# A long convolution with a gated dense block: products and inverse by 128 channels, D added ahead of the transposes, a new order

## The chip, the cores and the metric

The kernel runs on one core of a Trainium2 chip. The core has five engines that run side by side, each with its own queue of instructions: TensorE (PE in the profile, its weight loads PEld), VectorE (DVE), ScalarE (ACT), GpSimd (POOL) and SyncE (SP, which here only issues DMA transfers). Matmul results go to PSUM, from where DVE or ACT must copy them to SBUF before the PSUM tile can be used again; such a copy is called an eviction. The metric is the device time of one execution in microseconds (us), less is better. The inputs and the output are in HBM and of type bfloat16.

## The reference

Sequence length S = 2048, channels D = 640, hidden width F = 1728, batch 1.

```python
# part A: a gated long convolution
k_shift[s, d] = sum over t < 4 of k[s - 3 + t, d] * shift_k[d, 3 - t]
kv   = k_shift * v
y_f  = rfft(pad(kv, 4096)) * rfft(pad(ssm_k, 4096))      # along the sequence, by channel
y    = irfft(y_f)[:S].astype(bfloat16) + kv * ssm_D
A    = layernorm(q) * y                                   # no weights, eps 1e-5
h    = q + A
# part B: a dense block
u    = layernorm(h) @ w1 + b1                             # 640 -> 1728
act  = u * tanh(softplus(u))                              # Mish
out  = h + act @ w2                                       # 1728 -> 640
```

## The kernel before

The Fourier transform of length 4096 is taken in two stages, as matrix products with tables from HBM. The channels are split into five groups of 128 (`dc` or `m` = 0 to 4). Since y = irfft(...) + D·kv, D is added to the filter's first sample ahead of its transform.

**Order.** Every step is a named operation (`OP`) with an engine, its inputs and, where it needs one, a PSUM tile. The text `ORDER` (L25 to L60) lists all operations in the order in which they are emitted, and so sets the order of each engine's queue. `name@2` puts the operation in PSUM tile 2 of the four tiles of 128 x 1024 f32; a tile is free when the eviction of its former content is done. `name:d`, `:a` or `:p` puts an eviction (or a scaling) on DVE, ACT or POOL instead of its usual engine. An eviction is `ev` (L245), on ACT in L247 and on DVE in L249.

**The stages**, with the operations' names and lines:

- Loads (L302, on SP's queue): the filter rows (`d_n`, five of 512 KB), the first-stage table `g` (`d_g`), `k` and `v` (`d_k`, `d_v`), later q (`d_x`) and the weights. Small loads on ACT's queue: the constants (`d_cst` L255), the taps (`d_sk` L256), D as one row of 640 (`d_dr` L257). `wm` (L269) are nine warm-up matmuls.
- Filter: `k1pe` (L352) transposes a group's filter, 16 transposes of 128x128; `k1ev` evicts 2,048 columns; `dadd` (L359) adds D to the first sample, one row, on POOL; `s1kpe` (L374, L375) is the first stage, 16 pairs of matmuls into half tiles for each quarter of a group; `s1kev` evicts 1,024 columns.
- Short convolution and product: `ktpe` (L318) transposes k, `ktev` evicts it, `ktsh` (L322, POOL) shifts it by one, `kspe` (L334, L335) applies the taps (whose table is `coef` L286 and `wsh` L294), `kv` (L339, DVE) multiplies by v out of PSUM.
- Value: `s1vpe`, `s1vev` are the first stage of `kv`.
- Second stage (L400): `s2k` for the filter, all five groups in one matmul of 160 columns for each of 128 frequencies, evicted in tiles of 960; `s2v` for the value, by chunks of groups (`CHUNKS`: group 0, groups 1 and 2, groups 3 and 4), so with 32 or 64 columns.
- `sw` (L432): ten transfers of 512 KB from SBUF to SBUF that swap the real and the imaginary rows of the transformed filter. `pr` (L443, DVE): 20 products of filter and value, 2,048 elements a partition each.
- First inverse stage `i1pe` (L464), 20 operations of 16 matmuls, `i1ev` evicts 1,024 columns of each. An `i1pe` waits for all the products of its chunk.
- Second inverse stage `i2pe` (L519), for each of 16 tiles of 128 tokens (t): eight matmuls over 640 channels; `y` (ACT) evicts.
- Around it, by tile t: `ln1` (L495, L496, DVE) takes the statistics of q, `ln1p` (L500 to L502, POOL) the inverse deviation, `lnx` (L507 ACT or L509 POOL) the normalized q; `wb` (L522) and `h` (L524) multiply and add, `bn` (L528 to L530) takes h's statistics, `pow` (L532, POOL) the inverse deviation, `hc` (L534) scales; the result is transposed on PE (`trpe` L543, evicted by `trev`; tiles 0 and 1) or by a DMA (`tr` L547, the others).
- Dense block by units of tokens (`UNITS`: 256, 256, 512, 512, 512): `m1pe` (L570; L573 for the last 64 rows of F, block 13, whose two halves of tokens go to two halves of the partitions) and `hb` (L581, ACT, Mish); `m2pe` (L612, L620) for each tile of tokens, `res` (L635, DVE; L632 for the last tile, in two parts of 512 and 128 columns) adds h; `d_out` (L639) stores.

Ten of the 16 `ln1` stand ahead of the second inverse stage (two of them beside the products), and all 16 `i2pe` ahead of the first `m1pe`.

Of the kernel before, what the change touches and what calls it, by code (L numbers as in the profile page):

```python
# [11 lines left out]
ALU = mybir.AluOpType  # L12
BF16 = mybir.dt.bfloat16
# [3 lines left out]
S = 2048  # L17
# [20 lines left out]
s1vpe1_1@0 s1vev3_2 s1vpe1_0@1 s2v0pe_96@3 d_x0 s1vev1_0 pr0_32 sw1_00 s2v0pe_64@2 s1vev1_1 sw1_10 s2v0ev_96:d sw1_01 s1vpe2_0@1 s2v0ev_64 d_t2m
s1vpe2_1@0 pr0_96 sw2_00 s1vpe3_0@3 s1vev2_0 s2v0pe_0@2 d_x1 pr0_64 sw2_11 s1vev2_1 sw2_10 s2v0ev_0 ln1_3 s2v1pe_112@1 kspe4_1@0 s1vev3_0 sw2_01 pr0_0
ln1p3 s2v1pe_32@2 s2v1pe_16@3 s2v1ev_32 ln1_1 lnx3:p s2v1ev_16 s1vpe3_1@2 kv4_1 ln1p1 s2v1ev_112 s2v1pe_48@3 s2v1pe_64@0 s1vev3_1 s2v1ev_48:d lnx1:p  # L40
s2v1pe_96@1 s2v1ev_64 s2v1pe_0@2 pr1_48 s1vpe4_0@3 s2v1ev_96 s1vpe4_1@0 pr1_64 s2v1ev_0 s1vpe4_3@1 s1vev4_0:d s1vev4_1 s1vpe4_2@2 s1vev4_2 pr1_96
s2v1pe_80@0 i1pe0_0@3 s1vev4_3 pr1_112 s2v1ev_80 s2v2pe_32@2 pr1_16 i1ev0_0 s2v2pe_64@1 s2v2pe_0@0 pr1_32 s2v2ev_32 s2v2pe_96@3 s2v2ev_0 s2v2ev_64:d
s2v2pe_48@2 s2v2ev_96 s2v2pe_16@0 pr1_0 s2v2pe_80@1 s2v2ev_48 i1pe0_2@3 pr1_80 s2v2ev_16 s2v2pe_112@2 pr2_64 s2v2ev_80 i1pe0_1@0 pr2_48 d_w14
s2v2ev_112 d_x2 i1pe1_3@1 i1ev0_1 d_x3 pr2_32 d_w12 i1pe1_6@2 i1ev1_3 d_w10 pr2_80 d_w13 i1pe1_0@0 i1ev1_6 d_w11 pr2_16 i1pe1_5@1 i1ev0_2 i1pe1_4@2
pr2_96 i1ev1_0 i1pe0_3@3 i1ev1_4 pr2_112 i1pe1_2@0 i1ev1_5 pr2_0 i1pe1_7@2 i1ev1_2 i1pe1_1@1 ln1_2 i1ev0_3 i1pe2_6@0 ln1_4 i1ev1_7 ln1p2 i1pe2_5@3
i1ev1_1 ln1_12 ln1p4 i1pe2_7@2 i1ev2_5 ln1_0 i1pe2_0@1 lnx4:p i1ev2_6 ln1_8 i1pe2_1@3 lnx2:p i1ev2_7 i1pe2_3@0 ln1p0 i1ev2_0 i1ev2_1:d i1pe2_4@2
i1ev2_3 ln1_5 ln1p8 i1pe2_2@1 i1ev2_4 ln1_6 lnx0:p d_w2c i1ev2_2 d_w2b ln1_7 ln1p12 d_w2a i2pe0@3 i2pe1@0 y0 ln1p5 i2pe3@2 y1 wb0 i2pe9@1 y3 wb1 ln1p6
i2pe4@3 y9 h1 i2pe6@0 y4 bn1 i2pe7@2 y6 i2pe10@1 y7 h0 i2pe2@3 pow1 bn0 y10 i2pe12@0 ln1p7 y2 i2pe8@2 wb3 y12 i2pe11@1 pow0 hc1 i2pe13@3 y8 h3 trpe1@0
y11 lnx8:p i2pe5@2 hc0 y13 trev1 trpe0@1 wb2 i2pe15@0 trev0:a h2 i2pe14@3 bn3 y15 m1pe0_5@1 y5 bn2 pow3 m1pe0_4@0 hb0_5 w2z y14 hc3 m1pe0_2@2 ln1_11
# [111 lines left out]
def kernel(  # L161
# [25 lines left out]
    banks = [psum.tile([P, 1024], F32, name=f"ps{i}") for i in range(4)]  # L187
    big = ctx.enter_context(tc.tile_pool(name="big", bufs=1))

    cst = cpool.tile([P, 4 * P + 32], BF16, name="cst")  # L190
    sk_r = cpool.tile([32, 80], BF16, name="sk_r")
    coef = cpool.tile([P, 20, 7], BF16, name="coef")
    st1 = cpool.tile([P, NT, 2, 6], F32, name="st1")
# [487 lines left out]
```

## Time and profile before

| | us |
|---|---|
| three runs | 228.24, 310.08, 228.19 |
| median | 228.24 |
| profiled execution, its own time | 227.79 |
| its span (first to last instruction of the profile) | 226.0 |
| busy: PE, weight load, DVE, ACT, POOL | 214.5, 161.2, 133.8, 134.0, 56.6 |

The granted clock of TensorE is 1.00 in the whole span. Read the busy times by stretch, not over the span: PE, DVE and ACT are loaded differently in the convolution (to about 100 us) and in the dense block (after it). An instruction of PE, ACT or DVE begins before its predecessor's recorded end, so the time that one more instruction takes is the spacing of the starts, which is a little less than the recorded mean duration. "Idle before, releaser" names what ended the wait of an engine.

### The profile page before, as it was taken

What the parts mean: (1) busy time and instruction counts of PE and PEld (TensorE: products, weight loads), DVE (VectorE), ACT (ScalarE), POOL (GpSimd) and SP (SyncE); (2) the same over time, 40 slices, a digit from 0 to 9 for tenths busy, and PEclk for the clock granted to TensorE, in tenths of its full rate; (3) what the DMA queues carried; (4) which work ended last, traced back from release to release, by engine and by line L of the source; (5) the groups of instructions that cost most, each with busy time, mean ns of one, the idle gap of its engine ahead of it and who ended that gap; (6) DMA issues with size and microseconds to landing.
All of it is one profiled execution on the core that took longest, in us unless ns stands there. A gap on an engine that the chain in (4) does not pass through costs nothing.

```text
span 226.0 us, 6327 instructions
## 1 busy us (share of the span) xinstructions
PE 214.5 (95%) x2758; PEld 161.2 (71%) x2764; DVE 133.8 (59%) x240; ACT 134.0 (59%) x184; POOL 56.6 (25%) x103
## 2 busy tenths in 40 slices
PE   7999999998888999799899999999999999999994
PEld 2898999998778999788787654444667444666762
DVE  0576877898999999799999999500020200021041
ACT  2688899999999999999795004745500164300000
POOL 4377230000650018866847204100000000000000
PEclk9999999999999999999999999999999999999999
DMA  7999980049993959101301352820001100000102
GB/s 219 378 419 405 411 348 7 3 165 325 402 418 109 408 201 331 45 3 29 32 1 32 80 151 51 105 55 0 0 3 58 58 3 0 0 33 28 58 29 87
DMA packets 19421, 31.01 MB, mean 137 GB/s; under 512 B 10689, under 2 KB 14786, under 8 KB 18626
## 3 DMA queue, kind: packets, MB, share of 16 engines
q1 hardware_dynamic: 19104, 30.46, 39.5%
q8 instruction: 21, 0.34, 0.6%
q10 hardware_dynamic: 194, 0.15, 0.2%
q14 instruction: 6, 0.05, 0.1%
q0 software_dynamic: 96, 0.00, 0.0%
HBM read 20.45 MB, written 2.62 MB: 102 GB/s over the span
## 4 chain that ended last, share of the span: by engine, by line
PE 69%; ACT 15%; DMA 8%; DVE 3%; issue 2%; POOL 1%; SPq 1%; ACTq 0%; POOLq 0%; DVEq 0%
PE ps L612 25%; PE ps L570 22%; ACT uv L247 11%; DMA ra<-in_A_k_dram 5%; PE ps L400 5%; PE ps L464 5%; DMA ks<-in_A_ssm_k_dram 3%; PE ps L318 2%; PE ps L334 2%; PE ps L374 2%; ACT ks L581 2%; PE ps L335 2%; PE ps L620 1%; PE ps L573 1%; ACT ra L507 1%
## 5 line engine op out<-in xcount | busy, mean ns | idle before, releaser
L581 ACT ACTIVATE ks<-ps,b1s 128x512 bf16<-128x512 f32 (+1 forms) x70 | 35.9, 598 | 49.1 <-PE ps L570 16.9
L612 PE MATMUL ps<-ks 128*128 128x320 bf16 (+2 forms) x419 | 58.4, 299 | 0.1
L570 PE MATMUL ps<-G 128*128 128x512 bf16 (+1 forms) x320 | 57.6, 336 | 0.9 <-ACT ks L581 0.6
L612 PEld LDWEIGHTS <-ks 128*128 128x128 bf16 x420 | 40.2, 98 | 17.8 <-issue 1.3
L635 DVE TENSOR_TENSOR rb<-ps,rb 128x640 bf16<-128x640 f32 x15 | 11.9, 819 | 67.4 <-PE ps L620 65.1
L570 PEld LDWEIGHTS <-G 128*128 128x128 bf16 x325 | 31.1, 98 | 25.4 <-issue 2.0
L247 ACT CAST uv<-ps 128x1024 bf16<-128x1024 f32 x52 | 48.1, 1181 | 0.4 <-PE ps L375 0.2
L247 ACT CAST ks<-ps 128x960 bf16<-128x960 f32 (+3 forms) x50 | 41.1, 902 | 3.3 <-PE ps L375 1.3
L443 DVE TENSOR_TENSOR ks<-ks,uv 128x2048 bf16<-128x2048 bf16 x20 | 23.2, 1215 | 0.7 <-DMA ks<-ks 0.7
L400 PEld LDWEIGHTS <-G 128*128 128x128 bf16 x512 | 21.1, 96 | 3.3 <-issue 2.8
L464 PE MATMUL ps<-a_t,ks 128*128 128x128 bf16 x320 | 18.8, 219 | 0.3 <-ACT uv L247 0.3
L464 PEld LDWEIGHTS <-ks 128*128 128x128 bf16 x320 | 18.3, 113 | 0.5 <-issue 0.3
L500 POOL TENSOR_SCALAR ve<-mv 128x1 f32<-128x1 f32 x16 | 4.9, 308 | 46.7 <-DVE mv L496 45.6
L400 PE MATMUL ps<-uv,G 128*128 128x64 bf16 (+1 forms) x384 | 13.2, 187 | 2.1 <-ACT uv L247 1.8
L532 POOL TENSOR_TENSOR r<-ve,mhalf 128x1 f32<-128x1 f32 x16 | 10.2, 643 | 18.1 <-DVE ve L530 18.1
L528 DVE BATCH_NORM_STATS2 st<-rb 128x6 f32<-128x320 bf16 x32 | 14.1, 481 | 0.1
L339 DVE TENSOR_TENSOR ra<-ps,rb 128x1024 bf16<-128x1024 f32 x10 | 12.2, 1219 | 2.7 <-PE ps L335 2.7
L495 DVE BATCH_NORM_STATS2 st<-rb 128x6 f32<-128x320 bf16 x32 | 13.7, 471 | 0.0
L374 PE MATMUL ps<-cst,ra 128*64 128x128 bf16 x160 | 10.8, 220 | 1.3 <-ACT uv L247 1.1
L400 PE MATMUL ps<-ks,G 128*128 128x160 bf16 x128 | 11.2, 231 | 0.1
L249 DVE CAST ks<-ps 128x1024 bf16<-128x1024 f32 (+1 forms) x8 | 9.4, 1202 | 2.9 <-PE ps L375 1.9
L374 PE MATMUL ps<-cst,ks 128*64 128x128 bf16 x160 | 10.6, 220 | 0.4 <-POOL ks L359 0.4
(65 smaller groups left out, 259.3 us busy)
## 6 DMA issues: line engine op xcount, KB each, us to landing
ks<-ks SPq DMA_DIRECT2D x10, 512.0 KB, 7.2
G<-tab_g SPq DMA_DIRECT2D x8, 512.0 KB, 11.2
ks<-in_A_ssm_k_dram SPq DMA_DIRECT2D x5, 512.0 KB, 6.1
ra<-in_A_k_dram SPq DMA_DIRECT2D x4, 640.0 KB, 10.8
rb<-in_A_v_dram SPq DMA_DIRECT2D x4, 640.0 KB, 11.2
rb<-in_A_q_dram SPq DMA_DIRECT2D x4, 640.0 KB, 6.1
out_dram<-rb SPq DMA_DIRECT2D x15, 160.0 KB, 1.8
G<-in_B_w_dram SPq DMA_DIRECT2D x5, 432.0 KB, 7.9
```

The source lines that it names most:

```text
L247: nc.scalar.copy(o, i)
L339: nc.vector.tensor_tensor(kv_w[:, m, :, 8 * h:8 * h + 8, :], p_.f32().rearrange("p (l t d) -> p d t l", l=4, t=8), raw_v[:, 8 * h:8 * h + ...
L374: nc.tensor.matmul(ps[0:64, dgl, :], lhs, mc, start=True, stop=True)
L400: nc.tensor.matmul(p_.f32()[:, o:o + n], g_v[:, f, :], src[:, :, f, :], start=True, stop=True)
L443: nc.vector.tensor_tensor(o, o, v, ALU.mult)
L464: nc.tensor.matmul(pz[:, dgl, :], KS[:, k, b, :, l], a12[:, k, :], start=k == 0, stop=k == 1)
L495: nc.vector.bn_stats(st1[:, t, hh, :], xt(t)[:, hh * 320:(hh + 1) * 320])
L528: nc.vector.bn_stats(st2[:, t, hh, :], xt(t)[:, hh * 320:(hh + 1) * 320])
L570: nc.tensor.matmul(ph[:, o:o + w], w1[:, dc, fc * P:fc * P + P], lt[:, dc, 0:w], start=dc == 0, stop=dc == NDC - 1)
L581: nc.scalar.activation(hb[:, fc, 0:n], p_.f32()[:, i * 512:i * 512 + n], ACT.Mish, bias=b1s[:, fc:fc + 1], scale=1.0)
L612: nc.tensor.matmul(p_.f32()[:, o:o + n], lhs, w2[:, k, cols:cols + n], start=fc == 0, stop=single and fc == 13)
L635: nc.vector.tensor_tensor(x, p_.f32().rearrange("p (a d) -> p a d", a=2)[:, :, 0:320], x, ALU.add)
```

## The change

1. **D ahead of the transposes.** The identity for the transposes is no longer loaded with the constants, but made by POOL. D is loaded as 20 values for each of 32 groups of channels, repeated for four partitions; DVE picks its own value for each partition (`lane`, `dsel`, `dcol`) and adds it to the filter's first column before the transposes. The transposes begin with sample columns 1 to 15; column 0, which holds the sum, comes last. The five additions on POOL go.
2. **Halved first eviction.** The first filter group's eviction (`k1ev0`) is in two halves, and each quarter of its first stage waits for its half alone.
3. **Chunks** of the value's second stage: groups 0 to 2 (96 columns) and groups 3 and 4 (64 columns). That is 256 matmuls instead of 384, evicted in 13 tiles of 960 or 768 and 8 of 1,024 columns.
4. **Products and first inverse stage by group of 128 channels.** Still 20 products of 2,048 elements; an `i1pe` waits for the four products of its own group. The inverse's buffer is laid out by groups, so that `i2pe` has four matmuls (two of 512 columns, two of 128) instead of eight, over the same 1,280 columns.
5. **Split second inverse stage** for tiles 0 to 3: `i2a` (groups 0 to 3) waits for the evictions of these groups alone, `i2b` for the last group.
6. **Units 0 and 1 merged in part**: block 13 of F of both units is computed together in `m1pe1_6`, and the second dense layer of tiles 0 to 3 is done in one set that waits for both units.
7. **Last tile** in parts of 384 and 256 columns instead of 512 and 128.
8. **A new order of everything.** Of the `ln1`, four stand beside the value's stages (ahead of the products), four among the `i1pe`, two among the first `i2pe` and six beside the `m1pe` of units 0 and 1. Tiles 8 and 11 have their `i2pe` behind the `m1pe` of unit 1, the other 14 ahead of the first `m1pe`. More evictions are on DVE: for the filter's first stage 8 instead of 6, the value's first stage 6 instead of 4, `s2k` 6 instead of 2; `s2v` 2 instead of 3; one `ktev` moves from DVE to ACT.

```diff
-CHUNKS = [[0], [1, 2], [3, 4]]
+CHUNKS = [[0, 1, 2], [3, 4]]
...
-SW_PIECES = 2
+SW_PIECES = 1
...
+I2S = (0, 1, 2, 3)
+K1S = (0,)
...
+D_FIRST = True
+MERGE = True
+BY_DC = True
...
-    d_dr = OP("d_dr", "actq", emit=lambda e: nc.scalar.dma_start(d_row, A_ssm_D.unsqueeze(0)))
+    d_dr = OP("d_dr", "actq", emit=lambda e: nc.scalar.dma_start(dful[:], A_ssm_D.rearrange("(d n) -> d n", n=20).unsqueeze(1).to_broadcast([32, 4, 20])))
+
+    def emit_id(e):
+        nc.gpsimd.memset(ident, 0.0)
+        nc.gpsimd.affine_select(out=ident, in_=ident, compare_op=ALU.not_equal, fill=1.0, base=0, pattern=[[-1, P]], channel_multiplier=1)
+    o_id = OP("idn", "pool", emit=emit_id)
+    o_ln = OP("lane", "dve", [o_id], emit=lambda e: nc.vector.tensor_reduce(lane[:], ident.rearrange("p (d l) -> p l d", l=4), axis=AX.X, op=ALU.max))
...
     for b in range(NDC):
+        dad = OP(f"dadd{b}", ["dve", "pool"], [d_n[b], o_dc], emit=lambda e, b=b: (nc.gpsimd if e == "pool" else nc.vector).tensor_tensor(raw_n[b][:, 0:1], raw_n[b][:, 0:1], dcol[:, b:b + 1], ALU.add))
...
-            for t2 in range(NT):
+            for t2 in [*range(1, NT), 0]:
                 nc.tensor.transpose(o[:, t2, :], raw_n[b][:, t2:S:16], ident)
...
-            nc.gpsimd.tensor_tensor(k, k, d_row.rearrange("p (d m l) -> p m d l", m=NDC, l=4)[:, b], ALU.add)
...
-        nf = 32 if n == 32 else 16
-        prods.append([])
-        for f0 in range(0, P, nf):
...
+        for dc in dcs:
+            prods.append([])
+            for f0 in range(0, P, 32):
...
-            i1_pes.append(OP(f"i1pe{c}_{gi}", "pe", prods[c] + [d_a12], psum=p_, emit=pe))
...
+            i1_pes.append(OP(f"i1pe{dc}_{gi}", "pe", prods[dc] + [d_a12], psum=p_, emit=pe))
...
+        if t in I2S:
+            o_i2 = OP(f"i2a{t}", "pe", [x for x, c in i1_evs if c < 4] + [d_t2m], psum=p_, emit=lambda e, i2=i2: i2(e, [(0, 4)]))
+            o_i2 = OP(f"i2b{t}", "pe", [o_i2] + [x for x, c in i1_evs if c == 4], uses=[p_], emit=lambda e, i2=i2: i2(e, [(4, 5)]))
...
-            parts = [(0, 512), (512, 128)] if last else [(0, 320), (512, 320)]
+            parts = [(0, 384), (512, 256)] if last else [(0, 320), (512, 320)]
```

The part of the new order around the turn from the inverse to the dense block (names as above):

```
i1pe4_3@0 ln1_6 i1ev4_1 ln1p10 i1pe4_0@2 i1ev4_3:d i1ev3_0 b1pe@1 ln1p6 d_w2b i1ev4_0 i2a0@3 ln1_4 d_w2c i2a1@0 d_w2a
c_b1 w2z i2b0 i2b1 ln1_11 i2pe15@2 y1 i2a3@1 y0 i2a2@0 wb1 y15 i2b2 h1 i2b3 i2pe5@3 wb0 y2 i2pe14@2 h0 y3 bn0 i2pe13@0 y5 i2pe6@1 y14 i2pe7@3 bn1 pow0
y6 i2pe12@2 y7 i2pe4@1 wb2 pow1 y12 hc0 i2pe9@3 h2 y4 trpe0@2 hc1 wb3 trev0:a trpe1@1 bn2 lnx12:p trev1:a i2pe10@2 y13 m1pe0_5@1 h3 pow2 y10 bn3
```

206 lines of the change are left out of this document (114 added, 92 removed).

## The prediction

> **What bounds the kernel now.** I read the page first, then the busy time by stretch, the waits of the engines, the groups by shape and the timeline around the turn from the convolution to the dense layers. The page has the totals and the chain that ended last:
>
> ```profile
> span 226.0 us, 6327 instructions
> PE 214.5 (95%) x2758; PEld 161.2 (71%) x2764; DVE 133.8 (59%) x240; ACT 134.0 (59%) x184; POOL 56.6 (25%) x103
> ...
> PE 69%; ACT 15%; DMA 8%; DVE 3%; issue 2%; POOL 1%; SPq 1%; ACTq 0%; POOLq 0%; DVEq 0%
> ```
>
> PE's 95% is an average. The stretches (length, then busy time of PE, weight load, DVE, ACT, POOL) show two halves with different limits:
>
> ```profile
> 20.00:40.00 20.00, 19.44 (x363) 19.00 (x358) 16.10 (x14) 18.52 (x22) 4.00 (x6) 1.00 0.67 269
> ...
> 60.00:80.00 20.00, 17.52 (x412) 16.39 (x407) 19.97 (x19) 20.00 (x23) 4.97 (x6) 1.00 0.83 324
> 80.00:100.00 20.00, 18.63 (x304) 18.09 (x302) 17.89 (x44) 19.53 (x27) 13.36 (x30) 1.00 0.44 145
> 100.00:120.00 20.00, 19.12 (x191) 16.07 (x189) 19.31 (x53) 17.55 (x38) 12.60 (x26) 1.00 0.15 18
> 120.00:140.00 20.00, 19.95 (x137) 12.00 (x136) 19.39 (x57) 3.38 (x7) 6.76 (x11) 1.00 0.37 83
> ```
>
> Up to 92 us PSUM evictions are the limit: from 60 to 80 us ACT has no gap and DVE hardly one, while PE waits 2.5 us. From 120 us on PE is busy 19.95 of 20. So the second half (some 105 us of matmuls, which the change leaves as they are) moves as a block, and the gain is what the first half and the turn give. The timeline at the turn (start, length, engine, line, what):
>
> ```profile
> 58.46 34.01 ACT L247 CAST uv<-ps 128x1024 bf16<-128x1024 f32 x37 [0.20 <-PE ps L400]
> ...
> 70.38 1.21 DVE L249 CAST uv<-ps 128x1024 bf16<-128x1024 f32 x1
> 71.52 11.43 DVE L443 TENSOR_TENSOR ks<-ks,uv 128x2048 bf16<-128x2048 bf16 x10
> ...
> 74.19 16.64 PE L464 MATMUL ps<-a_t,ks 128*128 128x128 bf16 x288 [0.27 <-ACT uv L247]
> 90.66 0.49 PE L519 MATMUL ps<-uv,ra 128*128 128x128 bf16 x4
> 92.52 7.02 PE L519 MATMUL ps<-uv,ra 128*128 128x128 bf16 x100 [1.37 <-ACT uv L247]
> ...
> 102.15 3.98 PE L570 MATMUL ps<-G 128*128 128x256 bf16 x35
> ```
>
> The last product ends at 71.52 + 11.43 = 82.95, yet the first inverse stage (L464) runs to 90.8 and the second (L519) waits until 92.52 for ACT, which evicts without a break to 58.46 + 34.01 = 92.47. So before the change the first half ends with PE and ACT, and DVE, done with the products 8 us before, fills the time with layer norm statistics (L495).
>
> **The change, part by part.** Prices of one instruction, from the groups:
>
> ```profile
> L443 DVE TENSOR_TENSOR ks<-ks,uv 128x2048 bf16<-128x2048 bf16 x20 | 23.2, 1215 | 0.7 <-DMA ks<-ks 0.7
> L249 DVE CAST uv<-ps 128x1024 bf16<-128x1024 f32 x8 | 9.7, 1218 | 0.2 <-PE ps L464 0.2
> L400 PE MATMUL ps<-uv,G 128*128 128x64 bf16 x256 | 9.5, 192 | 2.1 <-ACT uv L247 1.8 <-DVE ra L339 0.2
> L400 PE MATMUL ps<-uv,G 128*128 128x32 bf16 x128 | 3.7, 177 | 0.0
> L495 DVE BATCH_NORM_STATS2 st<-rb 128x6 f32<-128x320 bf16 x32 | 13.7, 471 | 0.0
> L359 POOL TENSOR_TENSOR ks<-ks,rd 1x128 bf16<-1x128 bf16 x5 | 2.2, 443 | 7.3 <-DVE ks L249 5.7 <-ACT ks L247 1.6
> L573 PE MATMUL ps<-G 128*64 128x128 bf16 x20 | 0.9, 224 | 0.0
> ```
>
> Instructions overlap their successors, so I take the spacing: an ACT eviction of 1,024 columns costs 34.01 / 37 = 0.92 us, a DVE one 71.52 − 70.38 = 1.14, a product 11.43 / 10 = 1.14, a statistics pair with its aggregate about 1.0 (two of 0.47 and a small one).
>
> *Evictions.* The order gives DVE two more evictions of the filter's first stage (ks), two of the value's first stage and four of the joint second stage, and moves one transposed-k eviction to ACT; the value's second stage has 13 evictions of 960 and 8 of 1,024 columns, for 21 chunkwise ones of which some were small. ACT's eviction work up to the second inverse stage falls by about 4 us of 78. DVE's work up to the last product rises: eight evictions more (8.8), three statistics that now stand before the last product (3.0) and the small D operations (0.6), less one eviction of the value's second stage and the k one (2.3).
>
> *Second stage on the value.* 256 matmuls of 64 to 96 columns for 384 of 32 and 64: 9.5 + 3.7 = 13.2 busy before; by spacing about 11.0, and 9.0 after, since columns stay and 128 starts go. PE isn't the limit there, so it counts nothing by itself.
>
> *Last product.* DVE waits in 6 to 83 us were these (engine, line, waited for, total, times, longest):
>
> ```profile
> DVE ks L249 <- PE ps L352: 7.1, 2, 5.0
> DVE ra L339 <- PE ps L335: 2.7, 6, 0.6
> DVE ks L249 <- PE ps L375: 1.9, 2, 1.6
> DVE uv L249 <- PE ps L318: 1.4, 3, 0.7
> DVE ks L249 <- PE ps L400: 1.0, 1, 1.0
> DVE ks L443 <- DMA ks<-ks: 0.7, 1, 0.7
> DVE ks L249 <- PE ps L483: 0.5, 1, 0.5
> ```
>
> The 5.0 lie before its first eviction, so 10.3 us are idle among the work, which is 82.95 − 6.4 (the first eviction) − 10.3 = 66. With the sum above it is 76 after the change, 74.7 of it from k1ev1 on, which can start at about 8.4 (before it lie the taps' table and D). Following the order with the prices above, each instruction starting when its engine and its inputs are there, I find 1.7 us of idle time left, because DVE has more queued at every point: last product at 8.4 + 74.7 + 1.7 = 84.8, 1.9 later than before. The swaps (L432) are issued at about 52.6 instead of 47.5 and the first product is at about 61, where neither is late.
>
> *Inverse by 128 channels.* i1 of a group waits for its own four products alone. Sixteen of the 20 are then done before the last product ends, and four are left: 4 × 16.64 / 18 = 3.7, so the last i1 ends at 88.5 (before 90.8, because 18 of them stood behind 74.19). ACT is 4 us lighter and ends the last eviction at about 90.4. Here is the gain's source: i2 of tokens 0 and 1 does its first 512 columns (7.02 us for 12.5 tokens less the last one's latency is 0.545 a token, 1,024 of its 1,280 columns 0.43) ahead of that eviction, so that the second inverse stage stands as if begun at 90.4 − 0.86 = 89.55, against 92.52 less 0.27 for the four early matmuls = 92.25. That is 2.7 without a single unplanned wait; allowing 0.5 for those, **2.2**. What covers this is DVE: each us that DVE is late moves it one to one.
>
> *Turn to the dense layers.* The layer norm statistics of eight tokens come later, some between i2's. Tokens 0 and 1 go through y, wb, h, statistics, power on POOL, scaling, transposes:
>
> ```profile
> 93.73 1.02 DVE L522 TENSOR_TENSOR ks<-ks,ra 128x640 bf16<-128x640 bf16 x2 [1.28 <-ACT ks L247]
> ...
> 95.31 0.89 DVE L528 BATCH_NORM_STATS2 st<-rb 128x6 f32<-128x320 bf16 x2
> ...
> 96.55 0.48 DVE L524 TENSOR_TENSOR rb<-ks,rb 128x640 bf16<-128x640 bf16 x1
> ...
> 99.58 1.01 DVE L534 TENSOR_SCALAR rw<-rb,mv,r 128x640 bf16<-128x640 bf16 x1
> L532 POOL TENSOR_TENSOR r<-ve,mhalf 128x1 f32<-128x1 f32 x16 | 10.2, 643 | 18.1 <-DVE ve L530 18.1
> ```
>
> From the first wb to the end of the scaling are 6.9 us now. In the new order I count four elementwise steps of 0.48, two statistics of 96.55 − 95.31 = 1.24, a power of 0.64 and two scalings of 0.5 between the start of wb1 and the end of its scaling: 6.0, say 6.1. wb1 stands behind the statistics of tokens 4 and 11 on DVE. With wb1 at 92.2, scaling ends at 98.3, transposes and their eviction at 99.5, and m1 starts at 99.65, against 102.15. PE would be ready at 98.3 (14 × 0.545 for i2 from 90.05, and the transposes), so 1.35 is a stall. But it starts with two i2's (2 × 0.545 = 1.1) undone that were done before: the lead is 2.5 − 1.1 = **1.4**.
>
> *Behind it.* Between 100 and 120 us PE idles 20 − 19.12 = 0.9. Statistics of later tokens now go beside units 0 and 1: **−0.5**, between 0 and −0.9. Merging feature block 13 of the first two units makes of two times ten 128-column matmuls ten of 256: the columns stay, ten starts go; between 0 and half of L573's 0.9, I take **−0.13**. The joint second dense layer of tokens 0 to 3 then waits for both units, which costs nothing while PE has m1 work of unit 1 and the two i2's in between. The last token's final piece is 256 columns instead of 128: its matmuls were in front anyway, its addition and its store are longer:
>
> ```profile
> L632 DVE TENSOR_TENSOR rb<-ps,rb 128x512 bf16<-128x512 f32 x1 | 0.7, 691 | 2.2 <-PE ps L612 2.2
> L632 DVE TENSOR_TENSOR rb<-ps,rb 128x128 bf16<-128x128 f32 x1 | 0.3, 292 | 0.1
> ```
>
> By these, 256 columns take 0.42, so **+0.2** with the store.
>
> *D ahead of the transposes.* Five POOL additions of 0.44 leave the path from k1's eviction to the filter's first stage, and the D column is added before the last transpose. The price is the start: D's load has 128 rows of 40 bytes, the filter taps' load stands behind it on ACT's queue, and an identity made on POOL comes before the first transposes.
>
> ```profile
> sk_r<-in_A_shift_k_dram ACTq DMA_DIRECT2D x1, 5.0 KB, 4.2
> b1b<-in_B_b_dram POOLq DMA_DIRECT2D x2, 0.1 KB, 4.9
> ...
> 5.15 1.23 PE L352 MATMUL ps<-cst,ks 128*128 128x128 bf16 x16
> 8.23 0.24 PE L374 MATMUL ps<-cst,ks 128*64 128x128 bf16 x1 [0.42 <-POOL ks L359]
> ```
>
> Small loads take 4.2 to 4.9 us whatever their size, so D, issued at 1.1, lands at 5.3 to 6.0, and the first transposes go at about 5.9 instead of 5.15. Its eviction, halved, lets the first stage start at about 8.0 (8.23 before). No row shows the identity's operation; the nearest is L359's 0.44 on a smaller tile. I allow 0 to 3 us (seven such) and take 0, because POOL idles before L359 (7.3 us for its five) and the identity is its first job. The two rows show no cost by size (4.2 for 5 KB, 4.9 for 0.1 KB).
>
> The Trainium skill (DMA: Bandwidth & Descriptors, "Why small descriptors are slow (HBM only)") says that each descriptor carries a fixed overhead, which small ones don't amortize. By that, D's 128 runs of 40 bytes would be late, as in rival 3; no row of this trace has that form.
>
> Sum on the path: −1.4 − 0.5 − 0.13 + 0.2 = −1.8: span 224.2. The profiled run was 227.79, 1.8 more than its span, and 0.45 under the median of the runs: 224.2 + 1.8 + 0.45 = 226.4.
>
> **Rivals.** (1) *DVE becomes the bound* (slower). If DVE's gaps stay as they were, 10.3 instead of 1.7, the last product ends 8.6 later, at 93.4, and everything behind it too, which has no slack against DVE in the new order: 226.4 + 8.6 = 235.0. For it: most of those gaps were waits for PE, which stays in lockstep with two evicting engines over four PSUM tiles. Against it: more work is queued on DVE, and gaps shrink on the engine that becomes the bound. The whole is slower than before once the gaps exceed 1.7 + 1.8 + the 0.5 already allowed = 4.0.
>
> (2) *Everything fits* (faster). No unplanned wait (0.5), no stall at the turn (1.35), none of the other 0.4 between 100 and 120, and half of the 1.7 gone: 226.4 − 0.5 − 1.35 − 0.4 − 0.85 = 223.3. For it: ACT has lost 4 us of work. Against it: the chain of token 1 is serial, and the prices are those of full queues already.
>
> (3) *Late start.* D lands 3 us later than the small loads of before, or the identity takes 3. The transposes hold DVE's queue, since dadd0 stands before the evictions; 2 of the 3 us reach the end, as 1 is absorbed by k's rows and DVE's gaps: 228.4.
>
> (4) *The gain is eaten at the turn.* The statistics of tokens 4 and 11 and the power on POOL, behind other small POOL work, hold the first scaling 1.6 us longer: 228.0, no change.
>
> **How the numbers follow.** Two per cent is about what a measurement of this kernel can tell from no change: below 223.7 is faster, above 232.8 slower. Forecast: 0.45, with its own bounds 225.5 (0.4 + 0.5 less) to 227.4 (0.5 + 0.5 more). Rival 2: 0.25, of which 0.17 is below 223.7. Rivals 3 and 4: 0.09 and 0.08. Rival 1: 0.13, of which 0.09 over 232.8, as its gaps may be anything between. Four hundredths more go to faster from the forecast's own side, if DVE's prices fall where its queue is full. Faster 0.17 + 0.04 = 0.21; slower 0.09; same 0.70. The range takes in rivals 2, 3 and 4 and the lower third of rival 1's: 222.3 to 229.8.
>
> **What would show it.** Right: DVE's idle time among its work up to the last product under 4 us, last product at 84 to 86, first dense i2 at 89 to 91, m1 at 99 to 101, PE over 99% from there. Wrong: a first product past 63, DVE waiting for PE between 25 and 60 us as long as before, first-stage matmuls after 9.5, or a PE gap over 2 us between i2 and m1.

## The result, and the profile after

The changed kernel takes 235.41 us (median of four runs, 235.33 to 235.57), the kernel before 228.48 in the same comparison: a ratio of 1.0303, interval 1.0274 to 1.0332. It is slower, by about 6.9 us, where 226.4 was predicted. One of the four runs before took 310.08 us; the median of the other three is 228.24. The profiled run took 235.57.

The head of the page after, with the engines' shares of the chain that ended last:

```profile
span 233.4 us, 5947 instructions
...
PE 217.7 (93%) x2562; PEld 160.4 (69%) x2562; DVE 141.2 (60%) x253; ACT 130.6 (56%) x180; POOL 51.7 (22%) x100
...
PE 70%; ACT 14%; DVE 11%; DMA 2%; issue 2%; ACTq 1%; DVEq 0%
```

DVE's share of the chain went from 3% to 11%. The positions tell where the 7.4 us between the two spans arise (from the timelines, in us; starts, unless the row says end):

| | before | predicted | after |
|---|---|---|---|
| first transposes of the filter | 5.15 | 5.9 | 6.94 |
| first stage of the filter | 8.23 | 8.0 | 9.68 |
| joint second stage of the filter | 25.27 | – | 28.23 |
| first product | – | 61 | 65.72 |
| last product, end | 82.95 | 84.8 | 95.05 |
| first inverse stage, end | 90.8 | 88.5 | 99.09 |
| first dense matmul (m1) | 102.15 | 99.65 | 109.33 |
| span | 226.0 | 224.2 | 233.4 |

Three us are lost before 28 us, and the last product ends 12.1 later than before. Behind it nothing is lost; from m1 on (length, then busy time of PE, weight load, DVE, ACT, POOL, the granted clock), after and then before:

```profile
109.30:233.40 124.10, 121.12 (x821) 75.12 (x820) 49.87 (x128) 43.64 (x81) 21.62 (x43) 1.00 0.16 41
```

```profile
102.10:226.00 123.90, 120.11 (x821) 74.07 (x824) 50.25 (x129) 42.64 (x80) 20.34 (x37) 1.00 0.18 41
```

In the 124.1 us lie two second inverse stages that were ahead of m1 before, 1.25 us by their row in PE's timeline:

```profile
124.35 1.25 PE L525 MATMUL ps<-uv,ra 128*128 128x512 bf16 x8
```

From the end of the first inverse stage to the end of the span, turn and second half together, are 135.2 us before (226.0 − 90.8), 135.7 by the prediction and 134.3 after. So this part gained 0.9, more than forecast, and the loss lies wholly ahead of it.

**The products.** The timeline of DVE (start, length, line, what, and in brackets the idle time and what ended it) shows them start and stop:

```profile
65.72 1.23 DVE L455 TENSOR_TENSOR ks<-ks,uv 128x2048 bf16<-128x2048 bf16 x1 [0.54 <-ACT uv L256]
68.03 1.23 DVE L455 TENSOR_TENSOR ks<-ks,uv 128x2048 bf16<-128x2048 bf16 x1 [1.08 <-ACT uv L256]
71.19 1.23 DVE L455 TENSOR_TENSOR ks<-ks,uv 128x2048 bf16<-128x2048 bf16 x1 [1.94 <-ACT uv L256]
73.50 2.36 DVE L455 TENSOR_TENSOR ks<-ks,uv 128x2048 bf16<-128x2048 bf16 x2 [1.08 <-ACT uv L256]
76.94 15.99 DVE L455 TENSOR_TENSOR ks<-ks,uv 128x2048 bf16<-128x2048 bf16 x14 [1.08 <-ACT uv L256]
...
93.88 1.17 DVE L455 TENSOR_TENSOR ks<-ks,uv 128x2048 bf16<-128x2048 bf16 x1
```

ACT's timeline over the same stretch is its mirror image; these are evictions of the value's second stage (L256 is the eviction on ACT):

```profile
67.04 0.96 ACT L256 CAST uv<-ps 128x960 bf16<-128x960 f32 x1 [1.34 <-DVE ks L455]
69.34 1.82 ACT L256 CAST uv<-ps 128x960 bf16<-128x960 f32 x2 [1.35 <-DVE ks L455]
72.51 1.88 ACT L256 CAST uv<-ps 128x960 bf16<-128x960 f32 x2 [1.35 <-DVE ks L455]
75.95 4.62 ACT L256 CAST uv<-ps 128x960 bf16<-128x960 f32 x5 [1.57 <-DVE ks L455]
```

Each waits for the other: DVE idles about 1.1 us, a little more than an eviction (0.96), and ACT 1.35, a little more than a product (1.23). The waits between 62 and 82 us (engine, line, waited for: total, times, longest) sum it up, and the window beside them (fields as in the windows above) has the cost, DVE at 5.76 of 10:

```profile
PE ps L416 <- ACT uv L256: 6.2, 4, 1.7
DVE ks L455 <- ACT uv L256: 5.7, 5, 1.9
ACT uv L256 <- DVE ks L455: 5.6, 4, 1.6
```

```profile
66.00:76.00 10.00, 4.75 (x81) 4.26 (x78) 5.76 (x5) 4.71 (x6) 0.00 (x0) 0.68 0.70 260
...
9.78:95.05 85.27, 76.54 (x1565) 72.21 (x1566) 75.82 (x79) 70.10 (x77) 18.22 (x26) 0.93 0.65 248
```

From its first eviction to its last product DVE is idle 85.27 − 75.82 = 9.45 us. PE's granted clock falls in the same stretch, to 0.50 from 70 to 80 us. No run separates this from the waits, but neither DVE nor ACT waits for PE there.

A product that waits for an eviction it reads is no surprise; an eviction that waits for a product is. The value's transformed chunk lies in rows of 512 columns, four for each of 128 frequencies. An eviction of ten frequencies writes runs of 40 columns, a product of 32 frequencies reads runs of 128. The waits in the compiled program:

```
ACT  eviction of columns 400-439    waits for the product of group 0, columns 0-127
DVE  product of group 1, 0-127      waits for the eviction of columns 400-439
ACT  eviction of columns 200-239    waits for the product of group 1, 0-127
DVE  product of group 2, 0-127      waits for the eviction of columns 240-279
ACT  eviction of columns 280-319    waits for the product of group 2, 0-127
DVE  product of group 1, 128-255    waits for the eviction of columns 280-319
ACT  eviction of columns 440-479    waits for the product of group 0, 256-383
DVE  product of group 1, 256-383    waits for the eviction of columns 440-479
```

None of these pairs has a column in common: the program keeps the emitted order between tiles that don't overlap. That is the alternation in the two timelines, step by step. The evictions of the second chunk, in runs of 64 columns, of which two make one run of a product, have no such waits. Why the program treats runs of 40 and of 64 differently is not shown; that it does is.

**The start.** PE's timeline (L298 is `cfpe`, the matmul that brings the taps to their place; L370 the transposes):

```profile
6.82 0.19 PE L298 MATMUL ps<-sk_r,cst 32*128 32x80 bf16 x1 [1.71 <-DMA sk_r<-in_A_shift_k_dram]
6.94 2.27 PE L370 MATMUL ps<-ident,ks 128*128 128x128 bf16 x27
```

PE idles 1.71 us for the taps, which the transposes behind it don't need. Before the change `cfpe` (L281 there) stood behind the first transposes and started at 6.3. The taps' load is issued behind D's, at 1.86 us, and takes 4.9 (loads: bytes, then us from issue to landing); so D landed at 5.4 and the taps at 6.8:

```profile
dful<-in_A_ssm_D_dram ACTq DMA_DIRECT2D x1, 5.0 KB, 4.3
sk_r<-in_A_shift_k_dram ACTq DMA_DIRECT2D x1, 5.0 KB, 4.9
```

The clock (last but two of the columns) is then at half from soon after 8 us until nearly 12. Experiment 3, which fills the idle time, and experiment 6, which removes it, keep it at 1.00:

```profile
8.00:9.00 1.00, 1.00 (x14) 1.00 (x13) 0.05 (x1) 0.80 (x1) 0.86 (x1) 0.61 1.03 409
9.00:10.00 1.00, 1.00 (x15) 0.82 (x15) 0.22 (x1) 1.00 (x2) 1.00 (x1) 0.50 0.99 398
10.00:11.00 1.00, 1.00 (x24) 1.00 (x22) 1.00 (x2) 0.35 (x2) 1.00 (x2) 0.50 1.01 420
11.00:12.00 1.00, 1.00 (x30) 1.00 (x28) 1.00 (x2) 1.00 (x2) 1.00 (x1) 0.68 1.02 412
```

The third thing at the start is on DVE, D's additions (L364) of 128 elements, with the filter's evictions (L258) between them; and beside them POOL's four products for the taps' table (`wsh`, L311), 2.03 us each:

```profile
5.92 0.16 DVE L364 TENSOR_TENSOR ks<-ks,dcol 128x1 bf16<-128x1 bf16 x1
...
10.92 1.32 DVE L364 TENSOR_TENSOR ks<-ks,dcol 128x1 bf16<-128x1 bf16 x1
12.23 1.23 DVE L258 CAST ks<-ps 128x1024 bf16<-128x1024 f32 x1
13.37 0.90 DVE L364 TENSOR_TENSOR ks<-ks,dcol 128x1 bf16<-128x1 bf16 x1
...
17.59 0.15 DVE L364 TENSOR_TENSOR ks<-ks,dcol 128x1 bf16<-128x1 bf16 x1
```

```profile
8.14 8.14 POOL L311 TENSOR_TENSOR rw<-cst,coef 128x1120 bf16<-128x1120 bf16 x4 [4.33 <-DVE coef L303]
```

Alone an addition takes 0.16 us, beside POOL's it takes 1.32 and 0.90, while the evictions out of PSUM between them keep their 1.23. The Trainium skill (SBUF — State Buffer, "Who interferes with whom") says that a VectorE instruction with two SBUF inputs contends with a GpSimd instruction that reads SBUF, and that one with at most one SBUF input doesn't, outside the two-port modes. The rows agree: the additions have two inputs in SBUF, the evictions none.

That gives three suspects: the ordering of disjoint work, the taps ahead of the transposes, and the additions beside POOL.

### The profile page after: what moved, and what is told of

It reads as the page before. It is cut to its first block, busy times and chain, and to the rows that moved or that the text cites. A ratio compares the mean times of both kernels' runs of the same rounds, so it can differ in the third digit from the quotient of the medians.

```text
span 233.4 us, 5947 instructions
## 1 busy us (share of the span) xinstructions
PE 217.7 (93%) x2562; PEld 160.4 (69%) x2562; DVE 141.2 (60%) x253; ACT 130.6 (56%) x180; POOL 51.7 (22%) x100
## 4 chain that ended last, share of the span: by engine, by line
PE 70%; ACT 14%; DVE 11%; DMA 2%; issue 2%; ACTq 1%; DVEq 0%
PE ps L647 25%; PE ps L582 24%; ACT uv L256 13%; PE ps L416 5%; DVE ks L258 4%; PE ps L390 3%; DVE ks L455 3%; PE ps L335 2%; DMA sk_r<-in_A_shift_k_dram 2%; PE ps L351 2%; PE ps L370 2%; PE ps L352 1%; PE ps L473 1%; PE ps L589 1%; PE ps L655 1%
## 5 line engine op out<-in xcount | busy, mean ns | idle before, releaser
L604 ACT ACTIVATE ks<-ps,b1s 128x512 bf16<-128x512 f32 (+1 forms) x69 | 35.4, 603 | 48.4 <-PE ps L582 48.4
L256 ACT CAST uv<-ps 128x1024 bf16<-128x1024 f32 (+1 forms) x52 | 48.0, 1104 | 6.3 <-DVE ks L455 5.6
L582 PEld LDWEIGHTS <-G 128*128 128x128 bf16 x325 | 31.2, 98 | 24.7 <-issue 1.5
L256 ACT CAST ks<-ps 128x640 bf16<-128x640 f32 (+3 forms) x44 | 36.2, 886 | 9.1 <-PE ps L391 4.6
L416 PEld LDWEIGHTS <-G 128*128 128x128 bf16 x384 | 21.7, 105 | 7.5 <-issue 6.8
L416 PE MATMUL ps<-uv,G 128*128 128x96 bf16 (+1 forms) x256 | 13.6, 218 | 6.2 <-ACT uv L256 6.2
L258 DVE CAST ks<-ps 128x1024 bf16<-128x1024 f32 (+1 forms) x14 | 16.5, 1191 | 1.8 <-PE ps L391 0.9
L390 PE MATMUL ps<-cst,ks 128*64 128x128 bf16 x160 | 11.6, 230 | 1.2 <-DVE ks L258 1.0
L390 PE MATMUL ps<-cst,ra 128*64 128x128 bf16 x160 | 11.3, 220 | 1.0 <-ACT uv L256 1.0
L416 PE MATMUL ps<-ks,G 128*128 128x160 bf16 x128 | 11.7, 230 | 0.1
L356 DVE TENSOR_TENSOR ra<-ps,rb 128x1024 bf16<-128x1024 f32 x10 | 11.5, 1213 | 0.3 <-PE ps L416 0.3
```

Of the source, the lines that this page charges most:

```text
L256: nc.scalar.copy(o, i)
L258: nc.vector.tensor_copy(o, i)
L390: nc.tensor.matmul(ps[0:64, dgl, :], lhs, mc, start=True, stop=True)
L416: nc.tensor.matmul(p_.f32()[:, o:o + n], g_v[:, f, :], src[:, :, f, :], start=True, stop=True)
L582: nc.tensor.matmul(ph[:, o:o + w], w1[:, dc, fc * P:fc * P + P], lt[:, dc, 0:w], start=dc == 0, stop=dc == NDC - 1)
L604: nc.scalar.activation(hb[:, fc, 0:n], p_.f32()[:, i * 512:i * 512 + n], ACT.Mish, bias=b1s[:, fc:fc + 1], scale=1.0)
```

## The experiments

Ratios are to the kernel before in the same comparison (medians 227.99 to 228.53).

**1. Tiles of eight frequencies.** Runs of 32 columns; the order of the value's second stage, and of the products in it, is fitted to 16 evictions of 768 columns in place of 13. So the edit changes the tile and the order around it together.

```diff
-        nb = 512 // n
+        nb = 4 if n == 96 else 512 // n
```

> The changed kernel with the value's second stage of groups 0 to 2 evicted in 16 tiles of 8 frequencies (768 columns, runs of 32) instead of 13 of 10 (960 columns, runs of 40), and the order around the products fitted to it. Theory (products and evictions of that stage, which touch different data, are ordered against each other because runs of 40 don't fit the products' runs of 128): the alternation of ACT and DVE from 66 to 76 us goes (5.7 us of DVE waiting for ACT, 5.6 the other way), and with it the clock of 0.50 there: 235.4 - 6 to 7 = about 229. Rival (the swaps, which land from 60.9 to 72.9 us, hold the products): DVE then waits for the transfers instead, at most 2 us better, 233.5 or more.

231.84 us, ratio 1.0161 (1.0125 to 1.0198): between the two expectations, and nearer to the rival's (233.5) than to the theory's (229). Both had a part. No wait of an eviction of this stage for a product is left, in the program or in the trace. But there are new waits, on DVE (group 2's first product waits for its swap) and then on ACT, ahead of the evictions of the inverse, and the late start is still there:

```profile
68.59 19.39 DVE L456 TENSOR_TENSOR ks<-ks,uv 128x2048 bf16<-128x2048 bf16 x17 [1.49 <-DMA ks<-ks]
```

```profile
79.69 17.51 ACT L257 CAST uv<-ps 128x1024 bf16<-128x1024 f32 x19 [1.67 <-issue]
```

**2. Taps' load first**, D's behind it; `cfpe` behind the first transposes.

```diff
-d_n0 cz d_dr wm@0 small lane d_n1 d_sk d_n2 ... dsel dcol cfpe@1 dadd0 d_a12 k1pe0@2
+d_n0 cz d_sk wm@0 small lane d_n1 d_dr d_n2 ... dsel dcol dadd0 d_a12 k1pe0@2 cfpe@1
```

> The changed kernel with the taps' load ahead of D's on ACT's queue and the taps' matmul behind the first transposes on PE. Theory (the taps' matmul at the head of PE's queue waits for the taps, which land at 6.8, and the gap of 1.7 us makes the clock fall to 0.50 for 3 us): first transposes at 5.2 instead of 6.9, no fall of the clock, second stage of the filter from about 25.5 instead of 28.2: 235.4 - 3 = 232.4. Rival (the start is absorbed, because the filter rows and k land when they do): under 1 us, 234.5 or more.

234.32 us, ratio 1.0265 (1.0223 to 1.0307): a gain of 1.1 us, a third of what was expected. Now D comes late: the transposes start at 5.59, but the last of them, of the column that holds D, waits 1.16 us for DVE's addition.

**3. Thirteen warm-up matmuls** instead of nine, to tell the lateness from the clock.

```diff
-WARM = 9
+WARM = 13
```

> The changed kernel with 13 warm-up matmuls instead of 9, which reach to the taps' landing. Theory of the clock: transposes still at 6.9, but the clock stays 1.00, and the first stage of the filter gains about 1.5 us, of which the end sees 1 to 1.5: 234.2. Rival (the clock falls anyway, or PE isn't the limit there): 235.4.

235.3 us, ratio 1.0305 (1.0259 to 1.035): nothing gained. Yet the clock stayed up, as its window shows (1.00, in the last column but two):

```profile
8.00:12.00 4.00, 3.91 (x96) 3.68 (x95) 2.83 (x3) 3.63 (x4) 3.71 (x2) 1.00 1.02 411
```

The joint second stage still starts at 28.36 (28.23 without the edit), so PE's speed isn't what makes the start late. Half clock from 8 to 12 us costs less than the interval's 1 us, if anything.

**4. POOL's table products emitted later**, behind the additions.

```diff
-wsh0 k1ev1 ... dadd2 ... wsh1 dadd4 ... wsh3 k1ev4 ... wsh2 d_v3 dadd3
+k1ev1 ... dadd2 ... dadd4 ... k1ev4 ... d_v3 dadd3 wsh0 wsh1 wsh2 wsh3
```

> The changed kernel with POOL's four tap masks (2 us each) behind the last addition of D instead of among them. Theory (DVE's additions of D to one column, 0.16 us when POOL is idle, took 1.32 and 0.90 beside the masks): all five take 0.16, DVE is 1.9 us lighter before 18 us, of which the end sees 0.5 to 1.5: 234.4. Rival (hidden behind waits for PE): 235.4; slower if the shift of k, which stands behind the masks on POOL, comes late.

235.83 us, ratio 1.0338 (1.0297 to 1.0378). The edit did nothing: POOL has nothing else queued there, so it starts the products when the taps' table is there (7.97 us, 8.14 without the edit), wherever they are emitted. It tells nothing about the additions.

**5. The additions on POOL**, four of them ahead of the table's products on its queue, the fifth between the second and the third.

```diff
-dadd0 ... dadd1 ... wsh0 ... dadd2 ... wsh1 dadd4 ... wsh3 ... wsh2 d_v3 dadd3
+dadd0:p ... dadd1:p ... dadd2:p dadd4:p wsh0 wsh1 ... d_v3 s1kev2_0:d dadd3:p wsh2 wsh3
```

> The changed kernel with the five additions of D on POOL, four of them ahead of the tap masks and the fifth between two masks. In the run before, moving the masks behind the last addition in the order changed nothing, as POOL has its own queue and starts the masks when the taps are there. Theory (on DVE the third and fourth addition stand still while POOL makes masks, 1.3 + 0.7 us beyond their 0.16, and the first stage's evictions stand behind them): DVE's waits go, the filter's second stage begins 2 to 3 us earlier, at about 25.5: 235.4 - 2.5 = 232.9. Rival (those waits are covered by PE and PSUM): second stage at 28 as before, 235.4.

234.7 us, ratio 1.0287 (1.0231 to 1.0342): by itself little. The first transposes still wait for the taps (2.33 us in this run's profile); experiment 9 shows what the move is worth without that.

**6. `cfpe` behind the first transposes**, D's load first as in the change.

```diff
-dsel dcol cfpe@1 dadd0 d_a12 k1pe0@2
+dsel dcol dadd0 d_a12 k1pe0@2 cfpe@1
```

> The changed kernel with the taps' matmul behind the first transposes in PE's queue, and D's load still first on ACT's queue. Theory (the taps' place at the head of PE's queue costs the start): transposes at 5.3, all 16 done at about 6.4, since D is there at 5.4 and added at 5.9; first stage 1.5 us earlier than 9.7; clock 1.00. If the additions on DVE then still stand still beside the masks, the end sees only about 1 us: 234.4.

233.97 us, ratio 1.0243 (1.0199 to 1.0286). PE no longer waits for the taps:

```profile
5.33 1.93 PE L370 MATMUL ps<-ident,ks 128*128 128x128 bf16 x16
7.19 0.22 PE L298 MATMUL ps<-sk_r,cst 32*128 32x80 bf16 x1
```

The joint second stage starts at 26.58, 1.65 earlier. The additions on DVE take as much as without the edit, 2.9 us together for 2.7 (shortest, median and longest in ns, then the stretch):

```profile
L364 DVE TENSOR_TENSOR ks<-ks,dcol x5: 161/731/974, 6.0 to 16.0; 128x1 bf16<-128x1 bf16 x5
```

**7. 1, 5 and 6 together**, and the product that waited for its swap behind two other products.

```diff
-s2v0pe_96@0 pr2_0 s2v0ev_80 s2v0pe_104@3 pr1_32 s2v0ev_72 s2v0pe_112@2 pr0_64
+s2v0pe_96@0 s2v0ev_80 s2v0pe_104@3 pr1_32 s2v0ev_72 s2v0pe_112@2 pr0_64 pr2_0
```

> The tiles of 8 frequencies, the additions on POOL and the taps' matmul behind the transposes together, and the first product of the third group two places later, so that its swap, which held DVE for 1.5 us, has landed. Theory (the three costs add): 235.4 - 3.6 (tiles, as run) - 3 to 4 (start) - 0 to 1.5 = about 228, first products at 61, last at 86. If the start's gain is lost to the swaps' transfers or to the first inverse stage, 231.

228.91 us over ten runs, ratio 1.0003 (0.9976 to 1.003): the whole loss is made up. DVE's products run nearly without a break, and the last ends at 85.43 (84.8 was predicted for the change):

```profile
61.24 3.62 DVE L456 TENSOR_TENSOR ks<-ks,uv 128x2048 bf16<-128x2048 bf16 x3
65.04 18.26 DVE L456 TENSOR_TENSOR ks<-ks,uv 128x2048 bf16<-128x2048 bf16 x16 [0.18 <-ACT uv L257]
...
84.26 1.17 DVE L456 TENSOR_TENSOR ks<-ks,uv 128x2048 bf16<-128x2048 bf16 x1
```

But ACT ends its inverse evictions at 75.64 + 17.51 = 93.15, where 90.4 was predicted:

```profile
52.44 22.00 ACT L257 CAST uv<-ps 128x768 bf16<-128x768 f32 x27
75.64 17.51 ACT L257 CAST uv<-ps 128x1024 bf16<-128x1024 f32 x19 [1.19 <-issue]
```

**8. Group 1's products first**, so that the first inverse stage, and ACT with it, can start earlier; one more inverse eviction on DVE. The rest of the stretch is reordered to fit.

```diff
-pr0_0 ... pr1_0 ... pr1_32 ... pr0_64 pr2_0 ... pr1_64 ... i1ev4_2
+pr0_0 ... pr1_0 ... pr1_32 ... pr1_64 pr2_0 ... pr1_96 ... pr0_64 ... i1ev4_2:d
```

> The three repairs of the run before, and the second group's four products so early that its first inverse operations stand ahead of the value's last second-stage operations, and one more of the last inverse evictions on DVE. In the run before, ACT evicted the second stage until 74.4, waited 1.2 us, and then needed 17.5 us for 19 inverse evictions, so that the end of the inverse hung on ACT. Theory (ACT is the limit there): no gap on ACT (-1.2), one eviction less (-0.9): about 226.3, faster than the kernel before by 0.8%. Rival (PE's inverse matmuls or the products are the limit): 228.5, as the run before.

230.83 us, ratio 1.0084 (1.0054 to 1.0114): wrong, and slower than experiment 7. The inverse matmuls begin 0.5 us earlier than in experiment 7 (71.70 for 72.22), but then come in pieces: PE waits for ACT for up to 1.70 us, and ACT for PE, twice for more than 1 us:

```profile
80.93 1.01 ACT L257 CAST uv<-ps 128x1024 bf16<-128x1024 f32 x1 [1.95 <-PE ps L474]
83.26 9.26 ACT L257 CAST uv<-ps 128x1024 bf16<-128x1024 f32 x10 [1.31 <-PE ps L474]
```

In the run shown the clock is at about half between 78 and 82 us too, so part of these waits may be the clock's. The three of its seven runs at full clock take 229.28 to 230.02, and the seven such runs of experiment 7 take 228.02 to 229.45. So the order itself costs about 0.7 us by these medians (229.66 for 228.95).

**9. 5 and 6 without 1**: the start repaired, tiles of ten as in the change.

> The changed kernel with the two repairs of the start alone: the additions of D on POOL, the taps' matmul behind the first transposes; the tiles of 10 frequencies stay. Theory (each alone is covered by the other, 0.7 and 1.4 us; the start's cost is 3.3 us together, as the start of the filter's second stage moved from 28.2 to 24.9 in the run with all): 235.4 - 3.3 = 232.1, and the rest of the way to 228.4, 3.7, is the tiles'. Rival (the repairs only add, 2.1): 233.3.

232.36 us, ratio 1.0163 (1.0129 to 1.0197), as expected; against experiment 6 the move of the additions is worth 1.0243 − 1.0163 = 0.008, some 1.8 us. The additions now all take the same:

```profile
L365 POOL TENSOR_TENSOR ks<-ks,dcol x5: 193/194/196, 5.9 to 15.0; 128x1 bf16<-128x1 bf16 x5
```

The ordering is untouched, between 62 and 82 us:

```profile
DVE ks L456 <- ACT uv L257: 5.7, 5, 1.9
ACT uv L257 <- DVE ks L456: 5.6, 4, 1.6
```

With experiments 1 and 7 this makes a square: the start costs 1.0303 − 1.0163 = 0.014 with the ordering there and 1.0161 − 1.0003 = 0.0158 without it, the ordering 0.0142 and 0.016. Within the intervals (about 0.003 to 0.004 on each ratio, so up to 1 us) the two add up: 3.2 to 3.7 us each. The square isn't quite clean, as the corner of experiment 7 also has the product moved that waited 1.49 us for its swap in experiment 1.

**10. Experiment 8 without the split second inverse stage.**

```diff
-I2S = (0, 1, 2, 3)
+I2S = ()
```

> The first kernel of this set with the second inverse stage of tokens 0 to 3 not split. My prediction gave the split 0.86 us, two tokens' first 512 columns ahead of the last eviction. If so: 0.9 slower than the first kernel of this set. If the turn is held by token 1's chain on DVE and POOL: 0.3 to 0.5 slower, since only the first y counts.

229.64 us, ratio 1.0057 (1.0037 to 1.0077). The runs at full clock took 229.28 to 230.02 with the split (experiment 8) and 229.32 to 229.67 without. The split is worth nothing that can be measured in this order.

**11. Experiment 7 with another order of the inverse**: group 0's first matmuls ahead, ACT's evictions in the order in which PE finishes.

```diff
-s2v1ev_16 i1pe1_3@1 i1pe0_0@0 pr2_64 i1ev1_3 i1pe1_1@3 pr3_96 i1ev0_0 ...
+i1pe0_0@0 pr2_96 d_w13 s2v1ev_48 d_w11 i1pe1_1@3 s2v1ev_16 i1ev1_2 i1pe1_3@1 pr2_64 i1ev0_0 i1pe0_1@0 ...
```

> The run with all three repairs, and the first inverse stage in another order: first the operations whose PSUM tile and products are there, so that ACT goes from the last second-stage eviction (74.4) to the first inverse eviction without the gap of 1.2 us; products and engines as in that run. Theory (the end of the inverse hangs on ACT: 22.0 us of evictions before 74.4, 17.5 behind it): inverse evictions end at 91.9 instead of 93.2, m1 at 100.6, and the whole 1.2 less than the run with all three repairs: 227.2 to 227.6. Rival (the products or PE's matmuls hold it as well): no change, 228.4.

227.69 us over twelve runs, ratio 0.9975 (0.9954 to 0.9995): near what was expected, the best of the study, and 0.6 us faster than the kernel before, which is at the edge of what the interval can tell. ACT has one gap of 0.27 us from 52.23 to 92.02:

```profile
52.23 35.76 ACT L257 CAST uv<-ps 128x768 bf16<-128x768 f32 x42
88.26 3.76 ACT L257 CAST uv<-ps 128x1024 bf16<-128x1024 f32 x4 [0.27 <-PE ps L474]
```

**12. One more inverse eviction on DVE**, on top of 11.

```diff
-i1ev4_1
+i1ev4_1:d
```

> The kernel of e11 with one more of the last five inverse evictions on DVE, which had 2.4 us idle before its own one there. Theory (ACT is the limit, 0.92 us an eviction): up to 0.9 less than e11: 226.5. Rival (the last inverse matmuls end at 90.5 to 91.6 whatever ACT does, so the eviction behind them is what counts): no change to e11, or 0.3 more.

228.0 us, ratio 0.9978 (0.9952 to 1.0003): no change. ACT's last eviction starts after a wait of 0.75 us for PE instead, at 91.57: PE is what is late next.

## Why the prediction was wrong

*Last product* is the step that failed. It laid DVE's queue out with "each instruction starting when its engine and its inputs are there" and found 1.7 us of idle time; 9.45 came. An instruction starts when the program's waits let it, and these were taken to be the data it needs. The tiles of ten frequencies and the products of 32 put other waits there, 5.7 us of them on DVE; the other 3.7 are small waits, mostly for PE. That the diff's change of chunk (96 columns, so 512 // 96 = 5 frequencies in half a tile) makes runs that don't divide a product's was there to be read, and so were the waits in the compiled program. The price of DVE's work was nearly right: 75.82 busy from that first eviction on, where 74.7 were predicted from there, and the additions beside POOL are more than the difference. With the three repairs of experiment 7 the position came true, 85.43 for 84.8, in part by luck: from 7.9 us on DVE is idle for 4.4 us, not 1.7, but busy for only 73.1.

*D ahead of the transposes* failed on three counts. The step put the transposes at about 5.9 as if they waited for D alone; the new order puts `cfpe` ahead of them in PE's queue, where it waits for the taps, whose load it had named as standing behind D's, without a price. D's own load was priced well (landed at 5.4, for 5.3 to 6.0), and repaired the transposes start at 5.07 to 5.33, and with the additions on POOL too the first stage at 7.85 to 8.04, for 8.0 predicted. The additions were priced with their neighbours at 0.6 us as if alone; two of them took 2.2. And the cost of a late start was taken as partly absorbed (2 of 3 us in rival 3), while here it reaches the end whole: 3.0 us late at the joint second stage, and 3.2 to 3.6 us in experiment 9's square. The identity on POOL, allowed 0 to 3 us, is done at 1.29, after 0.20 for its memset and 0.29 for its affine select, well ahead of the transposes. From the Trainium skill's rule on small descriptors, named there, the prediction took that D's 128 short rows would be late; they landed in 4.3 us, like the other small loads. That is no test of the rule, and "4.2 to 4.9 us whatever their size" was read from too few rows: the constants, 104 KB, issued just before on the same queue, landed in 2.0.

*Inverse by 128 channels*, on which the sum's −1.4 rests, failed in its size: 2.2 us of gain were to come from ACT, "4 us lighter". ACT did get lighter, but not where it was the limit. Before and in experiment 11 (fields as above; ACT is the fourth busy time):

```profile
8.00:30.00 22.00, 21.16 (x471) 19.88 (x472) 15.92 (x16) 19.63 (x22) 11.45 (x12) 1.00 1.02 412
30.00:52.00 22.00, 21.96 (x495) 21.32 (x494) 17.87 (x15) 21.03 (x24) 1.61 (x3) 1.00 0.31 125
52.00:92.50 40.50, 35.52 (x810) 33.75 (x807) 39.61 (x56) 40.27 (x44) 13.85 (x25) 1.00 0.82 299
```

```profile
8.00:30.00 22.00, 21.32 (x484) 20.17 (x481) 18.85 (x17) 17.49 (x19) 10.49 (x10) 1.00 1.02 416
30.00:52.00 22.00, 21.91 (x458) 20.39 (x456) 21.35 (x23) 18.68 (x21) 3.08 (x6) 1.00 0.43 152
52.00:92.00 40.00, 35.72 (x703) 32.62 (x702) 37.65 (x50) 39.70 (x48) 12.07 (x27) 1.00 0.76 283
```

Until 52 us ACT has 40.66 − 36.17 = 4.5 us less work, but there PE is busy 43.1 to 43.2 of 44 in both, which makes PE and not ACT the likely limit; from 52 us on, where ACT has hardly a gap in both, it has 0.6 less. Before the change its last inverse eviction ended at 92.47, and in the best order tried at 92.02, for 90.4 predicted. The first inverse stage ends at 90.9 in experiment 11, and at 90.8 before: with all three faults repaired the convolution's new arrangement is worth nothing in the best order tried, and what experiment 11 gains comes from behind it (134.2 us from there to the end, for 135.2, in the profiled runs). The split's 0.86 (two times 0.43) within the step was nothing in experiment 10.

*Evictions*: the sums were right, as above. *Turn* and *behind it* together were to take 0.5 more than before from the end of the first inverse stage on, and took 0.9 less, 1.4 less than forecast; which of their terms made that was not tested. The last tile's addition of 256 columns took 0.425 us for 0.42.

Of the rivals, the first gave 235.0, and that its number came so near is luck. It was right that DVE's gaps would be the trouble, but its reason was wrong: it had DVE wait for PE, in lockstep over PSUM tiles; DVE waited for ACT, by an order that the data don't ask for, and this makes only half of the loss. The other half is a late start, of which it had nothing and rival 3, with 228.4, too little. Of the signs named, two came (first product past 63, first stage after 9.5); DVE's waits for PE between 25 and 60 us fell, from 4.9 us to 2.0.

## What to carry to other kernels

Where two engines write and read one buffer in tiles of different shapes, look at the waits of the compiled program. Here it kept an order between tiles that share no element where runs of 40 met runs of 128, in both directions, and none where runs of 32 or 64 did. When work is moved from one engine to another, count the saving only in the stretch where the first is the limit. And price a new load by all that stands behind the instructions that wait for it, in each engine's own queue: here the transposes stood behind a matmul that waited for the taps.

## What the runs showed of the hardware

- An addition of 128 single elements took 0.16 us alone and up to 1.32 beside POOL's products of 2.03 us; on POOL itself 0.19. So one tiny instruction in the queue of the evictions cost as much as an eviction (1.23).
- After 1.71 us of idle time PE's clock went to half soon after 8 us, and again at 70 us, where PE's longest wait was 1.7 us. The four windows from 8 to 12 us lost (0.39 + 0.50 + 0.50 + 0.32) = 1.7 us of full clock, that is 3.4 us at half. The Trainium skill (TensorE: Matmul & The Clock Gate, "What's actually happening") gives some 3.4 us of sustained activity until full clock; the trace agrees. At the start it cost nothing measurable at the end: with full clock (experiment 3) the joint second stage starts no earlier.
- Making the identity on POOL took 0.20 us of memset and 0.29 of affine select:

```profile
1.00 0.29 POOL L270 TENSOR_SCALAR_AFFINE_SELECT ident<-ident 128x128 bf16<-128x128 bf16 x1
```
